# A weight transfer issued in nine pieces, and a bank of another group for two sums

## The chip, the cores and the metric

The kernel runs on one core of one Trainium2 chip. What counts is the time of one execution on the device, in microseconds (us). It is one kernel for two layers, a sliding-window attention and a spectral mixing layer behind it, and reads 163.58 MB from HBM, nearly all of it the weights of the second layer.

## The reference

The inputs are q, k and v of shape (8, 8, 576, 64), in float32, two sets of 64 matrices of 512x512 (`w_r`, `w_i`, 64 MB each) and one matrix `w_ch` of 512x512.

```python
# attention: causal, each row sees the 64 latest positions
scores = where(0 <= i - j < 64, q @ k.T / sqrt(64), -1e9)
x = softmax(scores) @ v                 # to (8, 576, 512)
# spectral mixing, 64 lowest modes of 576 positions
X = rfft(x, axis=1);  Xr, Xi = X.real[:, :64], X.imag[:, :64]
Yr = einsum('bmd,mde->bme', Xr, w_r) - einsum('bmd,mde->bme', Xi, w_i)
Yi = einsum('bmd,mde->bme', Xr, w_i) + einsum('bmd,mde->bme', Xi, w_r)
y = irfft(Yr + 1j * Yi, n=576)          # the other modes are zero
u = x + y
out = u + maximum(u @ w_ch, 0)
```

## The kernel before

The order of all work is written out by hand (a manual schedule): each engine runs its instructions in the order in which the Python code emits them. Semaphores between engines and transfers are put in by the framework.

**The weights** are streamed in bf16, cast on the way by transfers that GpSimd issues. `steps` is the list of groups of modes. For the first `EARLY` = 10 groups of four modes a step takes half of the rows (`hb`), so there are 20 such steps, ten with `hb` 0 and then ten with `hb` 1. After them come 12 steps of two whole modes each for the groups 10 to 15, two steps a group. Each step needs two transfers, `wr` and `wi`, `wlist` holds them in order, and `load_weights(n)` issues as many as it is allowed to. A transfer of the first 20 steps goes out at L178: 128 partitions, each with 4 modes of 2x512 values, 2 MB in HBM and 1 MB as it lands. Those of the last 12 steps go out at L169 and are of the same size; the last one of all is cut in three. A transfer needs a free buffer: `ringA` (3), `ringB` (5, the first 20 steps alone) or one of several lent tiles (`x_sb`, `Yfour`, `XQ`, `Yall`), and a buffer is free when the matmuls that read it are done. GpSimd's queue also carries q, k and v (L247) and `w_ch` (L1087), each in its place among the weights.

**The matmuls** of a step stand at L198 (`mode_half`, the first 20 steps) and L216 (`mode_pair`), 8 or 16 for each transfer. They add up in a PSUM tile `psm` of group "m"; DVE copies the sum out (L686, L709).

**While the weights come in**, the attention runs (until about 160 us). From then on, between two halves of a step, a list of jobs (`jobs`, `advance`) does what can be done ahead: `x @ w_ch` for all rows (`x_jobs`: transposes L639, matmuls L646, copies L867), and at the end, when the modes of the first 14 groups are there, for each batch `b` its inverse transform: `batch_job` (transposes into "t" at L762, ACT's copy L763, matmuls L646, ACT's copy L767), and for batches 0 to 3 `early_jobs`: `early_u`, which makes rows of `u` ahead (matmuls L825 and L826, then DVE's add L832 for odd tiles and ACT's copy L836 for even ones), and `add_late` (L811, L813). After the last weights the rows of the output are finished and sent out.

**PSUM** has eight banks: groups "m" (2), "t" (2), "y" (1), "p" (1) and "z" (2). `bank(group)` hands out the banks of a group in rotation; a new tile waits for the readers of the one that had the bank before. The two even sums of a batch (tiles 0 and 2, one job) take the banks "y" and "p" for batches 0 and 1, and both banks of "t" for batches 2 and 3.

Of the kernel before, what the change touches and what calls it, by code (L numbers as in the profile page):

```python
# [26 lines left out]
def kernel(  # L27
# [10 lines left out]
    nc = tc.nc  # L38
# [10 lines left out]
    HALF = DM // 2  # L49
    NJ = 2  # L50
# [6 lines left out]
    def pool(name, bufs=1, **kw):  # L57
        opened.append(tc.alloc_tile_pool(name=name, bufs=bufs, **kw))
        return opened[-1]
# [32 lines left out]
    EARLY = 10  # L92
    yp = pool("yp", side="right", reuse_waits="tile")
# [8 lines left out]
    XA = XA[:, 0:(3 * NW + 2) * B * NMF].rearrange("p (s b m) -> p s b m", b=B, m=NMF)  # L102
    steps += [(grp, hb) for grp in (*range(EARLY, LAST), *range(LAST + 2, NGRP), LAST, LAST + 1) for hb in range(2)]
    ONES = 3, 0
    wlist = []
    for at, (grp, hb) in enumerate(steps):
        for ri in range(2):
            p = 4 * grp
            if (at, ri) == ONES:
                parts = [[(p, p + 1)], [(p + 2,)], [(p + 3,)]]  # L110
# [33 lines left out]
    def load_weights(n):  # L144
        nonlocal nload
        while nload < len(wlist):
            at, parts, hb, ri = wlist[nload]
            if 2 * n <= sum(len(ps) for ps in parts):
                return
            if nload in lent:  # L150
                w = lent[nload]
            else:
                open_to = "a" if at >= 2 * EARLY else "aby" if at < EARLY + 2 else "ab"
                h = min(open_to, key=lambda h: held[h][0] if len(held[h]) == room[h] else -1)
                if len(held[h]) == room[h]:
                    if held[h][0] not in spent:
                        return
                    held[h].pop(0)
                held[h].append(nload)
                if h == "y":  # L160
                    w = lentY
                else:
                    w = {"a": ringA, "b": ringB}[h].tile([128, 4, NJ, DM], BF16, name="wi" if ri else "wr", tag="wt")
            src = moe_w_i if ri else moe_w_r
            if at >= 2 * EARLY:
                w = w.rearrange("p (m h) j e -> p m (h j) e", m=2)
                p = parts[0][0]
                for m, k, lo, hi in ((0, 1, 0, NW), (1, 1, 0, NJ), (1, 1, NJ, NW)) if nload == len(wlist) - 1 else ((0, 2, 0, NW),):
                    nc.gpsimd.dma_start(  # L169
                        out=w[:, m:m + k, lo:hi],  # L170
                        in_=src[p + m:p + m + k].rearrange("m (p j) e -> p m j e", j=NW)[:, :, lo:hi])
                wtiles.update(((p + m, ri), w[:, m]) for m in range(2))
                nload += 1
                n -= 2
                continue
            to = 0
            for ps in parts:
                nc.gpsimd.dma_start(  # L178
                    out=w[:, to:to + len(ps)],
                    in_=src[ps[0]:ps[-1] + 1, HALF * hb:HALF * hb + HALF, :].rearrange("g (p j) e -> p g j e", j=NJ))  # L180
                for i, p in enumerate(ps):
                    wtiles[p, hb, ri] = w[:, to + i]
                to += len(ps)
            nload += 1
            n -= to
# [38 lines left out]
    with tc.manual_schedule():  # L224
# [177 lines left out]
        at = scratch[:, 3 * NTC * NM:3 * NTC * NM + NTC]  # L402
# [6 lines left out]
        for nm in ("k", "q", "v"):  # L409
            load(1, nm)  # L410
        LEAD = 4
        load_weights(LEAD)
        nc.gpsimd.iota(Kb, pattern=[[64, NBLK]], base=0, channel_multiplier=0,
                       allow_small_or_imprecise_dtypes=True)
# [82 lines left out]
        def early_step(it):  # L497
            nonlocal step
            grp = step
            psm = ps_m.tile([128, DM], FP32, name="psm", tag="misc")  # L500
            for ri in range(2):
                mode_half(psm, grp, ri)
                load_weights(due(it) - loaded())
            nc.scalar.copy(out=Yacc[grp], in_=psm)
            step += 1
# [4 lines left out]
        for it in range(-3, NU + 3):  # L510
# [23 lines left out]
            g = starts.get(it + 2)  # L534
# [3 lines left out]
            g = starts.get(it + 1)  # L538
            if g is not None and g + 2 < NG:
                load(g + 2, "v")  # L540
            if it >= 0:
                for f in trig[0:2]:
                    f()
                del trig[0:2]
            load_weights(due(it) - loaded())
        do_dft(NG - 1)
        while step < EARLY:
# [24 lines left out]
        def bank(h, shape=(128, DM), dtype=FP32, name=None):  # L572
            return banks[h].tile(list(shape), dtype, name=name or "ps" + h, tag="bank")
# [56 lines left out]
        def yrows(b):  # L630
            return Yall[:, b, :]
# [184 lines left out]

        def early_u(b, cs):
            def done(_):
                pus = [bank("yp"[j] if b < 2 and len(cs) == 2 else "t") for j in range(len(cs))]
                for c, pu in zip(cs, pus):  # L820
                    i = tile_of(b, c)
                    at = tiles[i][1][0][0]
                    halves = pu.rearrange("p (h e) -> p h e", h=2)
                    if c % 2 == 0:
                        nc.tensor.matmul(out=halves, lhsT=ident_bf, rhs=tiles[i][0], start=True, stop=False)  # L825
                    nc.tensor.matmul(out=pu, lhsT=trigI[:, at:at + 128], rhs=yrows(b), start=(c % 2 == 1),  # L826
                                     stop=True)
                for c, pu in zip(cs, pus):
                    i = tile_of(b, c)
                    if c % 2:  # L830
                        UE[i] = spare[2 * b + c // 2]
                        nc.vector.tensor_tensor(out=UE[i].rearrange("p (h e) -> p h e", h=2),  # L832
                                                in0=pu.rearrange("p (h e) -> p h e", h=2), in1=tiles[i][0], op=ALU.add)
                    else:
                        UE[i] = x_sb[:, c // 2, b].rearrange("p c e -> p (c e)").bitcast(FP32)
                        nc.scalar.copy(out=UE[i], in_=pu)  # L836

            jobs.append((lambda: None, done))
# [19 lines left out]
        def tile_of(b, c):  # L858
            return 9 * (b // 2) + 4 * (b % 2) + c
# [24 lines left out]
        ps, pu = {}, {}  # L884
# [251 lines left out]
        for g in (2, 3):  # L1136
            nc.sync.dma_start(out=Zall.bitcast(FP32)[rows, 2 * g:2 * g + 2],
                              in_=ZL.bitcast(FP32)[32 * g:32 * g + 32])
# [43 lines left out]
```

## Time and profile before

| | |
|---|---|
| median of 3 runs | 432.17 us (431.64 to 432.29) |
| the profiled execution | 432.25 us |
| its span in the profile | 430.4 us |
| granted TensorE clock, mean | 0.886 |
| PE / DVE / ACT / POOL busy | 328.2 / 239.5 / 182.6 / 103.4 us |
| bytes moved, mean rate | 93.28 MB, 217 GB/s |
| weight transfers at L178, issue to landing | 13.6 / 21.7 / 38.6 us (least, median, most) |

All times inside the kernel are counted from the start of the span. PE is TensorE's matmuls, DVE VectorE, ACT ScalarE, POOL GpSimd, SP SyncE. A row of the timeline gives the start, the duration, the engine, the line of the code and the operation with the tile that it writes and reads; in brackets at its end stands how long the engine had been idle and what ended that. A transfer's issue on POOL is a row of its own (`DMA_DIRECT2D`); the transfer itself lands later.

### The profile page before, as it was taken

How to read it: one execution, taken by the hardware profiler on the slowest of the kernel's cores; microseconds unless marked ns; L12 is line 12 of the kernel's file. 1: busy time of each engine (PE TensorE's matmuls, PEld its weight loads, DVE VectorE, ACT ScalarE, POOL GpSimd, SP SyncE). 2: the span in 40 equal slices, each digit the busy share in tenths (PEclk: the TensorE clock that was granted, in tenths of full speed). 3: DMA queues.
4: the chain of work that ended last, by engine and by line, in shares of the span. 5: the costliest groups of instructions: out<-in, count | busy, mean ns of one | idle time of the engine just before them, and what ended most of it. 6: DMA issues, size and time to landing. Idle time of an engine off the chain costs nothing.

```text
span 430.4 us, 11413 instructions
## 1 busy us (share of the span) xinstructions
PE 328.2 (76%) x4962; PEld 220.9 (51%) x5006; DVE 239.5 (56%) x509; ACT 182.6 (42%) x330; POOL 103.4 (24%) x153
## 2 busy tenths in 40 slices
PE   6888989898999999974317344677587657979994
PEld 3666767676767676652104122345464445445552
DVE  8588877877577776876103112132222223874995
ACT  6566757575666667532201101114131213423663
POOL 8223222222122141112112100011111111120894
PEclk8699999999999999998556868559986999999998
DMA  8999999999999999999999999999999999995698
GB/s 205 211 211 212 211 213 209 211 212 212 211 211 212 212 212 210 212 212 212 212 257 214 212 211 212 215 214 214 212 215 214 209 215 213 214 211 95 226 372 301
DMA packets 40818, 93.28 MB, mean 217 GB/s; under 512 B 2528, under 2 KB 2784, under 8 KB 40768
## 3 DMA queue, kind: packets, MB, share of 16 engines
q0 software_dynamic: 35056, 81.80, 98.7%
q1 hardware_dynamic: 5568, 10.62, 6.7%
q8 instruction: 39, 0.64, 0.5%
q10 hardware_dynamic: 144, 0.13, 0.1%
q14 instruction: 11, 0.09, 0.1%
HBM read 163.58 MB, written 9.44 MB: 402 GB/s over the span
## 4 chain that ended last, share of the span: by engine, by line
DMA 49%; PE 37%; issue 6%; ACT 3%; DVE 3%; POOL 1%; DVEq 0%; POOLq 0%
DMA wi<-in_moe_w_i_dram 29%; DMA wr<-in_moe_w_r_dram 19%; PE tr L260 6%; PE s L307 4%; PE s L319 3%; PE pt L327 3%; PE vb L272 3%; PE o L347 2%; PE s L299 2%; PE psm L216 2%; PE psz L646 2%; PE psm L198 1%; PE pst L901 1%; DMA vd<-in_k_dram 1%; PE psz L901 1%
## 5 line engine op out<-in xcount | busy, mean ns | idle before, releaser
L646 PE MATMUL psz<-wch,tr 128*128 128x512 f32 x176 | 63.2, 490 | 11.7 <-DMA wch<-in_moe_w_ch_dram 10.9
L867 DVE CAST xw<-psz 128x512 fp32r<-128x512 f32 x36 | 24.9, 692 | 80.7 <-PE psz L646 80.7
L311 DVE TENSOR_REDUCE mx<-s 128x4 fp32r<-128x512 f32 x72 | 49.5, 688 | 25.8 <-PE s L307 25.5
L614 ACT CAST tr<-ptx 128x512 fp32r<-128x512 bf16 x36 | 21.2, 590 | 92.1 <-PE ptx L639 92.1
L646 PEld LDWEIGHTS psz<-wch,tr 128*128 128x128 f32 x176 | 36.8, 232 | 19.6 <-issue 11.3
L321 ACT ACTIVATE p<-s 128x512 bf16<-128x512 f32 x72 | 39.7, 603 | 13.5 <-PE s L319 13.5
L198 PEld LDWEIGHTS <-XQ 128*32 128x32 bf16 x320 | 13.0, 175 | 44.9 <-issue 27.3
L307 PE MATMUL s<-kT,qT 64*64 64x128 bf16 (+1 forms) x576 | 29.4, 223 | 6.9 <-issue 6.9
L264 ACT COPY kT<-tr 128x576 bf16<-128x576 bf16 x32 | 23.2, 725 | 21.5 <-PE tr L260 21.5
L198 PE MATMUL psm<-wi,XQ 128*32 128x512 bf16 x144 | 14.5, 478 | 20.7 <-DMA wi<-in_moe_w_i_dram 20.7
L264 ACT COPY qT<-tr 128x576 bf16<-128x576 bf16 x32 | 23.3, 728 | 11.0 <-PE tr L260 11.0
L330 DVE COPY pts<-pt 128x1024 bf16<-128x1024 bf16 (+1 forms) x40 | 25.2, 630 | 4.2 <-PE pt L327 2.7
L307 PEld LDWEIGHTS <-qT 64*64 64x64 bf16 x576 | 18.2, 108 | 18.0 <-issue 17.6
L319 PE MATMUL s<-mx,ident_r 128*128 128x512 f32 x72 | 26.8, 445 | 0.0
L686 DVE TENSOR_TENSOR stg<-psm,Yfour 128x512 bf16<-128x512 f32 x10 | 6.9, 690 | 35.4 <-PE psm L198 32.3
L169 POOL DMA_DIRECT2D wr<-in_moe_w_r_dram x12 | 8.4, 697 | 73.4 <-PE psm L216 37.4
L178 POOL DMA_DIRECT2D wi<-in_moe_w_i_dram x18 | 13.6, 754 | 51.2 <-PE psm L198 34.4
L264 ACT COPY vT<-tr 128x576 bf16<-128x576 bf16 x32 | 23.3, 728 | 4.1 <-PE tr L260 4.0
L247 POOL DMA_DIRECT2D rawk<-in_k_dram x15 | 8.1, 538 | 70.5 <-PE tr L260 64.2
L327 PE MATMUL pt<-ident_bf,p 128*128 128x128 bf16 x288 | 23.3, 220 | 1.5 <-issue 1.3
L216 PEld LDWEIGHTS <-XQ 128*32 128x32 bf16 x256 | 9.4, 151 | 28.4 <-issue 26.0
L198 PE MATMUL psm<-wr,XQ 128*32 128x512 bf16 x120 | 11.9, 477 | 15.7 <-DMA wr<-in_moe_w_r_dram 15.1
(257 smaller groups left out, 678.2 us busy)
## 6 DMA issues: line engine op xcount, KB each, us to landing
wi<-in_moe_w_i_dram POOLq DMA_DIRECT2D x29, 1024.0 KB, 18.4
wr<-in_moe_w_r_dram POOLq DMA_DIRECT2D x27, 1024.0 KB, 17.0
out_dram<-ut SPq DMA_DIRECT2D x29, 256.0 KB, 2.7
rawv<-in_v_dram POOLq DMA_DIRECT2D x16, 288.0 KB, 15.0
rawk<-in_k_dram POOLq DMA_DIRECT2D x15, 288.0 KB, 13.1
rawq<-in_q_dram POOLq DMA_DIRECT2D x15, 288.0 KB, 13.1
x_sb<-in_moe_w_r_dram POOLq DMA_DIRECT2D x2, 1024.0 KB, 15.9
out_dram<-utx SPq DMA_DIRECT2D x6, 256.0 KB, 2.3
```

Of the source, the lines that this page charges most:

```text
L198: nc.tensor.matmul(out=psm[32 * g:32 * g + 32, :], lhsT=XQ[hb].rearrange("k s b m -> k (s b) m")[:, (3 * j + 1 - ri) * B:(3 * j + 5 - ri) ...
L260: nc.tensor.transpose(out=pt[ro, j, :], in_=raw[ro, TH * half + j, :], identity=ident_bf[ro, ro])
L264: nc.scalar.copy(out=to, in_=pt.rearrange("p j n -> p n j"))
L307: nc.tensor.matmul(out=s[ro, t, lo:128], lhsT=lq, rhs=kT[ro, 64 * n - 64 + lo:64 * n + 64], start=False, stop=True, skip_group_check=True)
L311: nc.vector.tensor_reduce(out=mx, in_=s, axis=AX.X, op=ALU.max, negate=True)
L319: nc.tensor.matmul(out=s, lhsT=ident_r, rhs=mx.unsqueeze(2).to_broadcast([128, 4, 128]), start=False, stop=True, skip_group_check=True)
L321: nc.scalar.activation(out=p[:, 4 * c2:4 * c2 + 4, :], in_=s, func=ACT_F.Exp, scale=EX_SCALE)
L327: nc.tensor.transpose(out=pt[:, t, :], in_=st[u]["p"][:, t, :], identity=ident_bf)
L330: nc.vector.tensor_copy(out=ps[:, 0:nt, :], in_=pt[:, 0:nt, :])
L614: nc.scalar.copy(out=tr, in_=pt)
L646: nc.tensor.matmul(out=pz, lhsT=tr[:, c, :], rhs=wch[:, c, :], start=(c == 0), stop=(c == NDCH - 1))
L867: nc.vector.tensor_copy(out=XW[i], in_=multiply(tr))
```

## The change

There are two edits, which have nothing to do with each other.

The `wr` transfer of step 14 (group 4, second half of the rows) is no longer one issue of 128 partitions. It becomes eight issues of two partitions each (0-1, 2-3, up to 14-15) and one of the partitions 16 to 127. The bytes and where they go are the same; the issues follow each other on GpSimd's queue, in the place of the one.

In `early_u` the two even sums of batches 2 and 3 take one bank of "t" and one of "m", not two of "t".

```diff
     ONES = 3, 0
+    IN_PAIRS, NPAIR = (EARLY + 4, 0), 8
     wlist = []
...
             to = 0
+            cuts = [*range(0, 2 * NPAIR, 2), 2 * NPAIR, 128] if (at, ri) == IN_PAIRS else [0, 128]
             for ps in parts:
-                nc.gpsimd.dma_start(
-                    out=w[:, to:to + len(ps)],
-                    in_=src[ps[0]:ps[-1] + 1, HALF * hb:HALF * hb + HALF, :].rearrange("g (p j) e -> p g j e", j=NJ))
+                of = src[ps[0]:ps[-1] + 1, HALF * hb:HALF * hb + HALF, :].rearrange("g (p j) e -> p g j e", j=NJ)
+                for lo, hi in zip(cuts, cuts[1:]):
+                    nc.gpsimd.dma_start(out=w[lo:hi, to:to + len(ps)], in_=of[lo:hi])
                 for i, p in enumerate(ps):
                     wtiles[p, hb, ri] = w[:, to + i]
                 to += len(ps)
...
         def early_u(b, cs):
             def done(_):
-                pus = [bank("yp"[j] if b < 2 and len(cs) == 2 else "t") for j in range(len(cs))]
+                pus = [bank(("yp" if b < 2 else "tm")[j] if len(cs) == 2 else "t") for j in range(len(cs))]
```

## The prediction

> **What bounds the kernel now.** I read the page first: its slices, its queues and the shares of the chain that ended last.
>
> ```profile
> DMA  8999999999999999999999999999999999995698
> GB/s 205 211 211 212 211 213 209 211 212 212 211 211 212 212 212 210 212 212 212 212 257 214 212 211 212 215 214 214 212 215 214 209 215 213 214 211 95 226 372 301
> q0 software_dynamic: 35056, 81.80, 98.7%
> DMA 49%; PE 37%; issue 6%; ACT 3%; DVE 3%; POOL 1%; DVEq 0%; POOLq 0%
> ```
>
> The DMA engines are full from the first slice to the 36th, at one rate. So until about 396 us the end is set by the weight stream, all of it on GpSimd's queue q0; the 34 us after that are PE's, DVE's and POOL's. A change in the stream moves the end by what it does to the stream's last landing.
>
> Next I read GpSimd's timeline around the split transfer, which is issued at 186.77 us.
>
> ```profile
> 178.85 0.75 POOL L178 DMA_DIRECT2D wr<-in_moe_w_r_dram  x1
> 186.03 0.74 POOL L178 DMA_DIRECT2D wi<-in_moe_w_i_dram  x1 [6.44 <-PE psm L198]
> 186.77 0.75 POOL L178 DMA_DIRECT2D wr<-in_moe_w_r_dram  x1
> 195.06 0.74 POOL L178 DMA_DIRECT2D wi<-in_moe_w_i_dram  x1 [7.55 <-PE psm L198]
> ...
> 200.27 0.86 POOL L178 DMA_DIRECT2D wi<-in_moe_w_i_dram  x1 [2.98 <-DMA wr<-in_moe_w_r_dram]
> 205.27 0.74 POOL L178 DMA_DIRECT2D wr<-in_moe_w_r_dram  x1 [4.15 <-DMA wi<-in_moe_w_i_dram]
> 210.21 0.74 POOL L178 DMA_DIRECT2D wi<-in_moe_w_i_dram  x1 [4.19 <-DMA wr<-in_moe_w_r_dram]
> 215.12 0.74 POOL L178 DMA_DIRECT2D wr<-in_moe_w_r_dram  x1 [4.17 <-DMA wi<-in_moe_w_i_dram]
> ```
>
> From 200 us on an issue waits for a DMA, not for a free buffer. In the program as built, every transfer from GpSimd waits for one of eight landing semaphores in rotation, so for the landing of the transfer eight places before it. The trace agrees: those landed at 199.74, 204.74, 209.68 and 214.59, and the issues above start 0.53 after each. At most eight transfers are in flight, whatever their size. PE's timeline shows three of these landings (PE starts 0.04 to 0.05 after them), and that a later wait is for wch:
>
> ```profile
> 204.79 1.11 PE L198 MATMUL psm<-wi,XQ 128*32 128x512 bf16 x8 [4.10 <-DMA wi<-in_moe_w_i_dram]
> 209.72 1.11 PE L198 MATMUL psm<-wr,XQ 128*32 128x512 bf16 x8 [3.28 <-DMA wr<-in_moe_w_r_dram]
> 214.63 1.11 PE L198 MATMUL psm<-wi,XQ 128*32 128x512 bf16 x8 [3.47 <-DMA wi<-in_moe_w_i_dram]
> 227.21 1.19 PE L646 MATMUL psz<-wch,tr 128*128 128x512 f32 x2 [10.94 <-DMA wch<-in_moe_w_ch_dram]
> ```
>
> Each transfer leaves sixteen landing marks in the trace, one for each engine. For the transfer that landed at 214.59 the first mark is at 209.20: eight engines lie within 1.34 of it, eight come 3.46 to 5.38 later. The late eight have the same rate as the others (4.95 us a transfer) and are late because the instruction fetches (q8, 0.88 to 0.98 us each, 39 of them) take turns on eight engines. Their work sets every "last landing".
>
> Last, the end of the chain of waits:
>
> ```profile
> 361.68 14.56 DMA wi<-in_moe_w_i_dram
> ...
> 376.28 0.69 PE psm L216 x16
> ...
> 386.79 0.59 ACT x_sb L836
> 387.39 0.04 issue
> 387.43 0.38 PE ptx L762 x4
> ...
> 395.52 0.80 PE psm L216 x16
> ```
>
> After the landing at 376.24 the chain runs over DVE, PE and ACT, and meets the stream again at its very end: the last piece lands at 395.84, and the last matmuls of L216, which PE began at 395.45, go on without a gap. The two are level there, so an earlier PE alone gains nothing, and a later landing is paid in full.
>
> **The change, part by part.** *The pairs.* One issue becomes nine, so eight more on POOL. Each costs about 0.53 (L178 with one row a partition: 0.53; with four: 0.75), in all 4.2 us, and POOL was idle for 7.55 before its next issue: the issue time itself is covered. The waits are not. In flight before the split transfer are the eight issued at 157.22, 159.93, 160.66, 168.38, 169.11, 178.12, 178.85 and 186.03, which landed at 179.21, 184.63, 189.87, 194.78, 199.74, 204.74, 209.68 and 214.59. Pair 1 waits for the first of these (and for its buffer, 186.77 as now), pair 2 for the second, pair 8 for the last. So pair 8 can't be issued before 214.59 + 0.53 = 215.12, and by then every whole transfer has left the queue. Behind it on POOL stand the piece of 112, the wi of 195.06, wch of 195.79, and all weights after them; PE waits for these. That is the cost: the stream runs dry.
>
> The restart, for the latest engine, which finished at 214.59: pair 8 is issued 215.12 to 215.65; the piece of 112 follows at 215.65 (it waits only for pair 1, long queued and landed by then or up to 0.6 later if that pair sat on a late engine). From issue to first packet there are two rows. The small copies Yall<-stg, issued at 398.72 into an idle queue, show their first packet at 399.83, 1.11 later; the first transfer of the kernel, issued at 1.74, shows it at 4.94, 3.20 later. I take the warm one and add 0.20, since the issue is that much longer (0.75 against 0.55): 216.96. The first packets of the kernel took up to 1.34 where the usual one takes 0.19; I take 0.4 for this (bounds 0 and 1.15): 217.4. Then 112 partitions are 7 for an engine instead of 8, 28 packets of 4.95/32 = 0.155: 4.33, so it lands at 221.7. The split transfer landed at 219.54. The stream is 2.15 late. Bounds: 215.57 + 1.11 + 4.33 = 221.0, so 1.5; and 215.65 + 3.20 + 1.15 + 4.33 = 224.3, so 4.8.
>
> The fixed cost of a queued transfer from GpSimd is put at about 2.0 us by the Trainium skill (DMA: Bandwidth & Descriptors, Anatomy of one DMA); by it the sum would be 215.65 + 2.0 + 4.33 = 221.98, so 2.4 late. No run here shows that figure by itself.
>
> Does the loss come back? The early engines lose 5.4 more, for they stood still since 209.2, but their lead was worth nothing: all sixteen start level at 217.4, and each of the eight late ones gets one more instruction fetch before 396 as it does now (233.7, 275.3, 299.9, 315.5, 335.2, 354.6, 374.2 and 393.9, in turn). From 219.54 to 395.84 the latest engine needs 176.3 us before and after. Starting level takes 0.5 off the landing at 376.24 (there a fetch hit an engine already late), but not off the last one. Refilling costs nothing: the next issues follow at 0.75 apart, each for 4.95 us of work, and their buffers are free, since PE has used everything up to 214.63 and waits. wch, landed at 227.08, comes at about 229.2, and PE waits that much longer at L646. So the last piece lands at about 398.0, and PE, long there, goes on 2.15 later.
>
> *The banks.* In the jobs of batches 2 and 3 the second even sum moves from "t" to "m". PE's order stays; two waits go. For batch 2 (ACT L836 at 379.36) DVE is busy without a break from 377.42 to 380.94, so nothing moves. For batch 3 the transposes at 387.43 waited for ACT's copy of 386.79 to 387.39; now they can follow the sums, at about 386.8, 0.6 sooner. The banks of "m" that it takes were read long before, and the next pair's sums, at 382.17, get the one that L709 read at 376.99. The cover for this 0.6 is the stream: with the last piece at 395.84 or later, PE only waits longer for it. I count 0; without that cover it would be 0.6 less.
>
> Sum: 432.25 (the profiled execution, 430.4 of span and 1.85 around it) + 2.15 = 434.4. The median of the runs is 0.08 lower, so 434.3.
>
> **The rivals.** *A, the pairs pile up on two engines.* Which engines serve two partitions, no row shows. I assumed that all eight pairs are through before the piece of 112 starts. If all eight go to the same two and one of these is a late one, that engine has 8 x 0.62 = 4.95 to do after 214.59, then 4.33 for its share of the 112: 223.9, 4.35 late, 436.5. It decides where 4.95 exceeds the dry stretch of 2.8. For it: eight of sixteen engines are late. Against: even then two early engines would have done it by 214.2.
>
> By the Trainium skill (DMA: Bandwidth & Descriptors, Why a DMA increments its semaphore by 16 and not by 1) two partitions run on two consecutive engines from a round-robin cursor, which spreads eight pairs over all sixteen; it also tells of direct copies with the rounded-up sixteenth of the partitions on each engine from the first on, which would put them all on the first two. No run here shows which holds.
>
> *B, no dry stretch.* If the wait for the landing eight places back does not bind pair 8, the pieces queue behind 214.59 as the whole did, the late engines do 7 partitions instead of 8 wherever a pair lands on an early one, and the last landing comes up to 0.62 sooner; PE's 0.6 from the banks then counts too. 431.6: not slower, and within the noise. It decides if the piece of 112 goes out before about 213.3 (214.59 less the 1.31 to its first packet). Against it: four issues in a row start 0.53 after exactly that landing.
>
> *C, the loss is absorbed.* If the end after 376 were PE's alone, a late stream would be hidden and the time stay at 432.2. Against: the last matmuls go on within 0.04 of the last landing, so the slack is nil.
>
> **How the numbers follow.** The dry stretch, 433.7 to 435.5: 0.70. A: 0.12. B and C, both inside the 0.2% (0.86 us, 431.3 to 433.0) that a measurement of this kernel can tell from no change: 0.10. Faster by more has no mechanism in these rows, since the late engines can't save more than one partition; 0.08 for what they don't show. The range 432.9 to 436.8 holds the first two cases and leaves out nearly all of the rest. Faster 0.08, same 0.10, slower 0.82.
>
> **What would show it.** In GpSimd's timeline: pairs issued at about 186.8, 187.3, 190.4, 195.3, 200.3, 205.3, 210.2 and 215.1, each but the first two 0.53 after a landing, and the piece of 112 at 215.7. A dip in the page's DMA and GB/s rows in the 20th and 21st slices; sixteen landing marks within about 1 us after it; wch at L646 at about 229.3; the last L216 about 2 us later. If the rows of GB/s show no dip there, the forecast is wrong; if the marks show two engines 2 us behind the rest, it is A.

## The result, and the profile after

| | before | after |
|---|---|---|
| median of the runs | 431.93 us (4 runs, 431.64 to 432.29) | 435.58 us (4 runs, 435.47 to 437.43) |
| the profiled execution | 432.25 us | 435.47 us |
| its span | 430.4 us | 433.7 us |
| granted TensorE clock, mean | 0.886 | 0.883 |

The ratio is 1.0094, with a 95% interval of 1.0065 to 1.0123: slower by 3.65 us, where 2.15 was forecast.

The lines of the code have moved by 1 to 4 (the transfer of L178 is L182 now, the matmuls of L198 are L200, L216 is L218, L646 is L648, L762 is L764). First the page: its slices (10.8 us each), its weight queue and the shares of the chain that ended last.

```profile
DMA  8999999999999999999699999999999999996698
GB/s 204 211 212 212 212 213 209 211 212 211 211 212 211 212 212 210 212 212 212 119 202 249 211 212 212 213 215 215 214 215 214 215 213 215 215 214 137 218 365 308
q0 software_dynamic: 35632, 81.80, 98.0%
DMA 46%; PE 35%; issue 9%; DVE 3%; ACT 3%; POOL 2%; DVEq 0%; POOLq 0%
```

The hole in the stream is the 20th slice: 119 GB/s where 212 is usual. The peak that stood in the 21st slice before (257) is in the 22nd now (249). It is no catching up: it is the slice in which wch comes in, which lands as many bytes in 2.5 us as a weight transfer in 4.95, and it moved with wch. The bytes are the same, in 576 more packets. `issue`, time in which the chain waits for nothing that the profile shows, rises from 6% to 9% of the span.

GpSimd's timeline from the first pair on (start, duration, engine, line, operation; in brackets the idle time before and what ended it):

```profile
187.21 0.74 POOL L182 DMA_DIRECT2D wi<-in_moe_w_i_dram  x1 [6.43 <-PE psm L200]
187.94 1.11 POOL L182 DMA_DIRECT2D wr<-in_moe_w_r_dram  x2
190.08 0.54 POOL L182 DMA_DIRECT2D wr<-in_moe_w_r_dram  x1 [1.03 <-DMA Yall<-in_moe_w_r_dram]
194.99 0.54 POOL L182 DMA_DIRECT2D wr<-in_moe_w_r_dram  x1 [4.37 <-DMA wi<-in_moe_w_i_dram]
199.94 0.54 POOL L182 DMA_DIRECT2D wr<-in_moe_w_r_dram  x1 [4.42 <-DMA wr<-in_moe_w_r_dram]
204.95 0.54 POOL L182 DMA_DIRECT2D wr<-in_moe_w_r_dram  x1 [4.47 <-DMA wi<-in_moe_w_i_dram]
209.88 0.54 POOL L182 DMA_DIRECT2D wr<-in_moe_w_r_dram  x1 [4.39 <-DMA wr<-in_moe_w_r_dram]
214.80 1.25 POOL L182 DMA_DIRECT2D wr<-in_moe_w_r_dram  x2 [4.38 <-DMA wi<-in_moe_w_i_dram]
216.04 0.79 POOL L182 DMA_DIRECT2D wi<-in_moe_w_i_dram  x1
```

Every pair from the third on waits for a landing, the last for the wi of 187.21, which lands at 214.51. The row of 214.80 is two issues, pair 8 and, at 215.33, the piece of 112. The wi behind it, which had gone out at 195.06 before, goes out at 216.04.

What PE meets, in its timeline:

```profile
214.56 1.11 PE L200 MATMUL psm<-wi,XQ 128*32 128x512 bf16 x8 [3.48 <-DMA wi<-in_moe_w_i_dram]
231.20 2.04 PE L648 MATMUL psz<-wch,tr 128*128 128x512 f32 x4 [14.99 <-DMA wch<-in_moe_w_ch_dram]
```

The last whole transfer comes when it did (214.63 before). wch comes 3.99 later than before (227.21), and PE's idle time ahead of it grows from 10.94 to 14.99.

The end of the chain of waits (start, duration, what):

```profile
365.52 14.66 DMA wi<-in_moe_w_i_dram
380.22 0.69 PE psm L218 x16
...
394.55 2.09 PE psz L648 x8
396.67 0.59 ACT Zall L769
397.30 0.50 PE psz L813
397.81 0.61 PE psm L218 x16
398.84 0.83 PE psm L218 x16
```

The chain is the one of before, 3.94 later at 380.22 and 3.32 later at the last L218 (398.84 against 395.52). The landing marks say the same of the stream: the last piece is there at 399.19, against 395.84.

### The profile page after: what moved, and what is told of

Read it like the earlier page. It is cut to its first block, busy times and chain, and to the rows that moved or that the text cites. A ratio compares the mean times of both kernels' runs of the same rounds, so it can differ in the third digit from the quotient of the medians.

```text
span 433.7 us, 11428 instructions
## 1 busy us (share of the span) xinstructions
PE 328.8 (76%) x4962; PEld 221.1 (51%) x5006; DVE 239.2 (55%) x509; ACT 182.4 (42%) x330; POOL 107.6 (25%) x161
## 4 chain that ended last, share of the span: by engine, by line
DMA 46%; PE 35%; issue 9%; DVE 3%; ACT 3%; POOL 2%; DVEq 0%; POOLq 0%
DMA wi<-in_moe_w_i_dram 34%; DMA wr<-in_moe_w_r_dram 11%; PE tr L262 6%; PE s L309 4%; PE s L321 3%; PE pt L329 3%; PE vb L274 3%; PE o L349 2%; PE s L301 2%; PE psz L648 2%; PE psm L218 2%; PE psm L200 2%; DMA vd<-in_k_dram 1%; PE pst L903 1%; PE px L372 1%
## 5 line engine op out<-in xcount | busy, mean ns | idle before, releaser
L648 PE MATMUL psz<-wch,tr 128*128 128x512 f32 x176 | 62.9, 489 | 15.9 <-DMA wch<-in_moe_w_ch_dram 15.0
L648 PEld LDWEIGHTS psz<-wch,tr 128*128 128x128 f32 x176 | 36.9, 233 | 23.7 <-issue 15.4
L200 PEld LDWEIGHTS <-XQ 128*32 128x32 bf16 x320 | 13.1, 176 | 43.7 <-issue 28.2
L200 PE MATMUL psm<-wi,XQ 128*32 128x512 bf16 x144 | 15.3, 495 | 20.8 <-DMA wi<-in_moe_w_i_dram 20.8
L170 POOL DMA_DIRECT2D wr<-in_moe_w_r_dram x12 | 8.4, 697 | 75.3 <-PE psm L218 41.5
L182 POOL DMA_DIRECT2D wr<-in_moe_w_r_dram x23 | 15.7, 683 | 34.1 <-DMA wi<-in_moe_w_i_dram 13.2
L218 PEld LDWEIGHTS <-XQ 128*32 128x32 bf16 x256 | 9.2, 150 | 28.7 <-issue 27.0
L200 PE MATMUL psm<-wr,XQ 128*32 128x512 bf16 x120 | 12.4, 479 | 14.0 <-DMA wr<-in_moe_w_r_dram 13.3
```

The lines of the kernel that those rows point to most:

```text
L200: nc.tensor.matmul(out=psm[32 * g:32 * g + 32, :], lhsT=XQ[hb].rearrange("k s b m -> k (s b) m")[:, (3 * j + 1 - ri) * B:(3 * j + 5 - ri) ...
L648: nc.tensor.matmul(out=pz, lhsT=tr[:, c, :], rhs=wch[:, c, :], start=(c == 0), stop=(c == NDCH - 1))
```

## Experiments

All times are medians; the last column but one is the ratio to runs of the kernel before on the same chip (their medians: 432.07 to 432.23 us). "Split lands" is the last landing mark of the step-14 `wr`, in one piece or many, and "last piece" that of the last weights.

| | us | ratio (95%) | split lands / last piece |
|---|---|---|---|
| before | 431.93 | | 219.54 / 395.84 |
| after | 435.58 | 1.0094 (1.0065 to 1.0123) | 223.52 / 399.19 |
| banks alone | 431.79 | 0.9992 (0.9981 to 1.0003) | not split / 395.31 |
| pairs alone | 435.92 | 1.0081 (1.0059 to 1.0103) | 223.41 / 399.10 |
| seven issues | 432.35 | 1.0003 (0.9991 to 1.0016) | 219.44 / 395.85 |
| eight issues | 435.22 | 1.0061 (1.0040 to 1.0082) | 222.73 / 398.89 |
| eight equal pieces | 431.96 | 0.9999 (0.9989 to 1.0008) | 219.79 / 395.36 |
| cut at two steps | 439.77 | 1.0176 (1.0161 to 1.0191) | 223.23, then 269.47 / 403.10 |
| ten transfers cut | 437.24 | one run | / 400.94 |
| held whole | 435.53 | 1.0071 (1.0049 to 1.0093) | 223.24 / 399.09 |
| held whole, then a gap | 437.20 | 1.0101 (1.0079 to 1.0122) | 223.76 / 400.66 |

In ten of the eleven profiled executions the span ends 34.4 to 34.6 us after the landing of the last piece (with the pairs alone 35.1). So what a kernel loses is what its weight stream loses.

My theory: at most eight of GpSimd's transfers are in flight, small pieces take the places of large ones, the queue runs dry, and the restart is the loss. The rivals were that the banks matter, that the pairs do harm by themselves (as nine issues, or by piling up on two engines), and that the engines' lost lead, not the restart, is what costs.

**Banks alone**: the kernel before with this one edit.

```diff
-                pus = [bank("yp"[j] if b < 2 and len(cs) == 2 else "t") for j in range(len(cs))]
+                pus = [bank(("yp" if b < 2 else "tm")[j] if len(cs) == 2 else "t") for j in range(len(cs))]
```

> The banks alone, the transfer whole. My theory (the loss is the dry stretch of the weight stream): no change, 431.3 to 432.4, since PE and the last landing stand level at the end; the transposes of batch 3 at L764 (387.4 in the kernel before) start some 0.6 us sooner and PE waits longer for the last piece. Rival (the banks carry part of the loss of 3.65 us, by a new wait for a bank of group m): slower by 1 us or more.

PE's timeline of this kernel:

```profile
386.54 0.39 PE L762 MATMUL ptx<-ident_bf,Yall 128*128 128x128 bf16 x4
394.57 1.22 PE L216 MATMUL psm<-wi,XL 128*32 128x256 bf16 x16
```

The transposes that stood at 387.43 start 0.89 sooner and with no idle time before them, so the wait for ACT's copy is gone. The last matmuls start 0.88 sooner too (395.45 before) and then take 1.22 instead of 0.87, since they wait in mid-row for the last piece. They end at 395.79, 0.48 after the last piece (395.31), as they did before (396.32, with the piece at 395.84): the stream sets the end of both. The profiled span is 429.8. The interval of the ratio holds 1: no change that this measurement can tell.

**Pairs alone**: the changed kernel with the old banks.

```diff
-                pus = [bank(("yp" if b < 2 else "tm")[j] if len(cs) == 2 else "t") for j in range(len(cs))]
+                pus = [bank("yp"[j] if b < 2 and len(cs) == 2 else "t") for j in range(len(cs))]
```

> The pairs alone, the banks as before. My theory: the whole of the loss, 435.0 to 436.2, with the dip of the stream between 209 and 218 us. Rival (banks carry part of it): under 434.7.

435.92, and the intervals of this and of both edits overlap. The whole loss is the pairs'. PE's timeline has one thing more:

```profile
391.33 0.38 PE L764 MATMUL ptx<-ident_bf,Yall 128*128 128x128 bf16 x4 [0.46 <-ACT x_sb L838]
399.36 0.69 PE L218 MATMUL psm<-wi,XL 128*32 128x256 bf16 x16
```

The old wait for ACT is back, and the last matmuls start only after the last landing (399.10) and end 0.95 after it. In the ten other kernels they end 0.48 or 0.49 after it. So with the old banks PE ended some 0.5 us behind the stream in this execution; the times do not tell the two kernels apart (435.92 and 435.58).

**Seven and eight issues**: the same partitions cut less often. With seven, the large piece takes the place before the last whole one lands; with eight, it has to wait for that landing.

```diff
# seven issues
-            cuts = [*range(0, 2 * NPAIR, 2), 2 * NPAIR, 128] if (at, ri) == IN_PAIRS else [0, 128]
+            cuts = [0, 2, 4, 6, 8, 12, 16, 128] if (at, ri) == IN_PAIRS else [0, 128]
# eight issues
+            cuts = [0, 2, 4, 6, 8, 10, 12, 16, 128] if (at, ri) == IN_PAIRS else [0, 128]
```

> The same 16 partitions cut in 2, 2, 2, 2, 4, 4, then the 112: seven issues for nine, banks as in the changed kernel. My theory (at most eight transfers in flight): the piece of 112 then waits for the landing at about 209.6 and goes out at about 210, before the late engines are done at 214.5, so the late engines never stand still: 431.3 to 432.6, no dip below about half in the DMA row. Rival (each small piece costs the stream something of its own, 4 us over eight pieces): 434 to 435.

> One issue more than the kernel called seven: pieces of 2, 2, 2, 2, 2, 2, 4, then the 112. My theory: the piece of 112 waits for the last whole transfer, the landing at about 214.5, and goes out at about 214.8, some 0.5 us sooner than with nine issues: 434.6 to 435.4, so nearly all of the loss comes with this one issue. Rival (a price for each piece): halfway between, about 434.7 with seven at 434.2.

GpSimd's timeline of the kernel with seven issues, the large piece and the transfer behind it:

```profile
209.65 0.72 POOL L182 DMA_DIRECT2D wr<-in_moe_w_r_dram  x1 [4.38 <-DMA wr<-in_moe_w_r_dram]
214.87 0.78 POOL L182 DMA_DIRECT2D wi<-in_moe_w_i_dram  x1 [4.50 <-DMA wr<-in_moe_w_r_dram]
```

The same of the kernel with eight:

```profile
214.79 0.72 POOL L182 DMA_DIRECT2D wr<-in_moe_w_r_dram  x1 [4.33 <-DMA wr<-in_moe_w_r_dram]
215.50 0.78 POOL L182 DMA_DIRECT2D wi<-in_moe_w_i_dram  x1
```

And the GB/s of the page, first with seven issues, then with eight:

```profile
GB/s 209 212 211 211 211 212 212 211 211 211 212 211 212 212 212 211 212 212 212 188 223 221 212 212 212 215 214 215 214 214 215 215 214 213 215 214 130 225 375 299
```

```profile
GB/s 203 211 212 211 212 211 211 211 212 212 211 212 211 212 213 210 212 212 212 126 216 242 212 212 212 215 214 216 214 214 214 214 215 214 215 214 129 219 375 299
```

One issue more moves the large piece from 209.65 to 214.79 and costs 2.87 us (435.22 less 432.35); the ninth adds nothing that can be told. So it is neither the number of issues nor the two-partition pieces, but the place in the rotation that the large piece gets. Seven are free because the large piece then enters a queue in which the late engines still have nearly five microseconds of work (the wi ahead of it lands at 214.32). The early engines do fall back: the first landing mark of the large piece comes at 216.48, where that of the whole transfer came at 214.16 before, and their lost lead costs nothing at the end. The next wi lands 0.87 late (225.43 against 224.56), 0.48 of this is still there at the landing of 385.89 (385.41 before), and at the last piece it is gone; where it goes is told below.

**Eight equal pieces**: as many issues as the kernel that lost 3 us, but of 16 partitions each.

```diff
-            cuts = [*range(0, 2 * NPAIR, 2), 2 * NPAIR, 128] if (at, ri) == IN_PAIRS else [0, 128]
+            cuts = [*range(0, 129, 16)] if (at, ri) == IN_PAIRS else [0, 128]
```

> The split transfer as eight pieces of 16 partitions, banks as in the changed kernel: as many issues as the kernel called eight (435.2 us), and its last piece too can go out only after the landing at about 214.5. My theory (the late engines must run dry for a loss): at 214.5 they still have seven pieces, 4.3 us of work, so they don't stand still: 431.5 to 433.0. Rival (the number of places taken is what counts, wherever the bytes are): 434.8 to 435.6.

GpSimd's timeline:

```profile
209.70 0.51 POOL L182 DMA_DIRECT2D wr<-in_moe_w_r_dram  x1 [4.43 <-DMA wr<-in_moe_w_r_dram]
214.61 0.51 POOL L182 DMA_DIRECT2D wr<-in_moe_w_r_dram  x1 [4.41 <-DMA wi<-in_moe_w_i_dram]
215.56 0.76 POOL L182 DMA_DIRECT2D wi<-in_moe_w_i_dram  x1 [0.45 <-PE psm L200]
```

The last piece goes out as late as the large one did with eight unequal cuts (214.61 against 214.79), and the time is that of the kernel before. Each of the seven pieces issued earlier held an eighth of the work, so the late engines were still busy with them when the eighth was issued. What counts is the work in the eight places, not how many they are.

**Cut at two steps**: the `wr` of step 18 is cut in the same way as that of step 14.

```diff
-            cuts = [*range(0, 2 * NPAIR, 2), 2 * NPAIR, 128] if (at, ri) == IN_PAIRS else [0, 128]
+            cuts = [*range(0, 2 * NPAIR, 2), 2 * NPAIR, 128] if (at, ri) in (IN_PAIRS, (EARLY + 8, 0)) else [0, 128]
```

> A second transfer (step 18, wr) is cut like the first, eight pairs and 112; the queue runs dry again some 47 us later, now with engines that stand nearly level. My theory (each dry stretch costs its restart, 3 to 4 us): 438.0 to 439.8. Rival (the loss of the first is the lead of the early engines, which can be lost only once): 435.6 to 436.6.

GpSimd's timeline at the second place:

```profile
255.76 0.54 POOL L182 DMA_DIRECT2D wr<-in_moe_w_r_dram  x1 [4.37 <-DMA wr<-in_moe_w_r_dram]
260.86 1.25 POOL L182 DMA_DIRECT2D wr<-in_moe_w_r_dram  x2 [4.56 <-DMA wi<-in_moe_w_i_dram]
```

The pattern repeats. The last whole transfer lands at 260.58, the piece of 112 goes out at 261.39 and lands at 269.47, where the next whole transfer would have landed at 260.58 + 4.95 = 265.53: 3.94 late. The first is 3.69 late here (223.23 against 219.54) and 3.98 in the changed kernel. The time is 4.19 over that of after, and the last piece comes 3.91 later. At the second place the sixteen engines were already within 1.6 us of each other, so there was no lead left to lose. The rival "lost lead" is refuted; each dry queue costs its restart.

**Ten transfers cut**, to learn which engines are the late ones: the `wr` and `wi` of steps 12 to 16 each go out as four pieces of eight partitions by modes, and one of 112.

```diff
-    IN_PAIRS, NPAIR = (EARLY + 4, 0), 8
+    SKEW = EARLY + 2, EARLY + 7
...
-                for lo, hi in zip(cuts, cuts[1:]):
-                    nc.gpsimd.dma_start(out=w[lo:hi, to:to + len(ps)], in_=of[lo:hi])
+                parted = [(0, 8, 0, 4), (8, 16, 0, 1), (8, 16, 1, 3), (8, 16, 3, 4), (16, 128, 0, 4)]
+                for lo, hi, m, k in parted if SKEW[0] <= at < SKEW[1] else [(0, 128, 0, len(ps))]:
+                    nc.gpsimd.dma_start(out=w[lo:hi, to + m:to + k], in_=of[lo:hi, m:k])
```

> For a version that beats both: the ten weight transfers of steps 12 to 16 are issued as 8 partitions of four modes, 8 of one, the same 8 of two and of one, and the 112, banks as in the changed kernel. If a piece of eight partitions goes to eight consecutive engines and the next piece to the other eight, one half of the engines gets 0.31 us less work a transfer and the other 0.31 more, 3.1 us in all. If the eight late engines are the relieved half: the last landing about 2.5 to 3 us sooner and 429 to 430. If they are the loaded half: 434.5 to 435.5, and the reverse would gain. If late and early engines are mixed in both halves, or pieces go elsewhere: 432 to 435.5, with marks that spread further.

437.24 in a single run, 400.94 for the last piece. Five issues a transfer leave some 1.6 transfers in the eight places, and the stream ran thin (165 to 202 GB/s in five slices, where 212 is usual). The engines did come closer together, but by the early ones falling back. It doesn't tell the halves apart: a miss for its purpose, and one more case of the eight places.

**Held whole**: the sum above had been off in its restart, and this kernel measures the restart by itself. The `wr` of step 14 is one issue again, but GpSimd first copies a column of the wi before it into a small new tile (`hush`, 128x64), and so waits for the same landing as pair 8.

```diff
-            cuts = [*range(0, 2 * NPAIR, 2), 2 * NPAIR, 128] if (at, ri) == IN_PAIRS else [0, 128]
+            cuts = [0, 128]
+            if (at, ri) == IN_PAIRS:
+                nc.gpsimd.tensor_copy(out=hush[:, 0:1], in_=wtiles[4 * steps[at - 1][0], steps[at - 1][1], 1][:, 0, 0:1])
```

> No pieces at all: the wr of step 14 goes out whole, but GpSimd first copies one column of the wi before it (the transfer that lands at 214.6), so that the issue waits for that landing as pair 8 did. Banks as in the changed kernel. Theory (the loss is the dry queue, not the pieces): issued at about 214.8; from issue to last landing the piece of 112 took 8.19 us in the changed kernel, and one partition more an engine is 0.62, so it lands at about 223.6, 4.0 late, and the time is 435 to 436.5. Rival (the pieces add to it): the restart goes as I forecast, first packet 1.31 to 1.41 after the issue, 0.4 of ramp, 4.95 of work: landed at about 221.5, 2.0 late, time 433.5 to 434.3.

GpSimd's timeline:

```profile
186.36 0.74 POOL L185 DMA_DIRECT2D wi<-in_moe_w_i_dram  x1 [6.44 <-PE psm L203]
214.72 0.18 POOL L181 CAST hush<-wi 128x1 f32<-128x1 bf16 x1 [27.62 <-DMA wi<-in_moe_w_i_dram]
215.21 0.75 POOL L185 DMA_DIRECT2D wr<-in_moe_w_r_dram  x1 [0.30 <-issue]
215.94 0.75 POOL L185 DMA_DIRECT2D wi<-in_moe_w_i_dram  x1
```

435.53: 3.30 over its own runs of before, without a single small piece; the interval of the ratio overlaps that of the changed kernel. The first sixteen packets start 1.45 to 1.74 after the issue (216.66 to 216.95). With 4.95 of work behind the first packet the transfer would be there at 216.66 + 4.95 = 221.61; the first engine is done at 222.60, the median at 222.92 and the last at 223.24. So here the ramp is 1.0 to 1.6 us, 1.3 at the median. The early packets show it: the first sixteen take 0.21 to 0.81 us and single later ones up to 1.15, where the usual one takes 0.173.

**Held whole, then a gap**: the same, and behind the held issue GpSimd does 16 small memsets before it issues anything else.

```diff
                     nc.gpsimd.dma_start(out=w[lo:hi, to:to + len(ps)], in_=of[lo:hi])
+                if (at, ri) == IN_PAIRS:
+                    for _ in range(16):
+                        nc.gpsimd.memset(hush, 0.0)
```

> As hold, and GpSimd then does 16 small memsets (some 2.3 us) before it issues the next transfers, so that the held one is alone in the queue while it starts; its 4.95 us of work cover the gap, if the next is issued by 218. If what slows the restart is the issues that follow at 0.75 us each (they use the same queue), the held transfer lands 1 to 2 us sooner than in hold and the time is that much less, 433.5 to 434.5. If the slow start is the transfer's own, it lands within 0.3 us of hold's and the time is the same as hold's or up to 1 us more.

GpSimd's timeline, then the page's GB/s:

```profile
215.16 0.75 POOL L185 DMA_DIRECT2D wr<-in_moe_w_r_dram  x1 [0.30 <-issue]
215.89 3.31 POOL L188 MEMSET hush<- 128x64 f32 x16
219.54 0.74 POOL L185 DMA_DIRECT2D wi<-in_moe_w_i_dram  x1 [0.34 <-issue]
```

```profile
GB/s 206 211 211 212 211 212 212 210 212 212 211 213 210 212 212 211 212 213 211 100 187 257 211 212 212 214 213 215 214 215 215 213 216 212 216 213 137 214 372 303
```

Alone in the queue the held transfer is no faster: its median engine is done at 222.81 (222.92 without the gap), its last at 223.76. That is 0.52 later than without the gap, outside the 0.3 that I had named, and not the 1 to 2 us sooner of the other case. So the issues that follow don't make the restart slow. The gap itself came out longer than planned, 3.31 us and not 2.3, and the next issue, at 219.54, was 3.3 us ahead of the median engine's end of work. Even so there is a second hole: 15 to 22 packets start in each half microsecond from 222.5 to 223.5, where some 50 are usual, and single ones take 1.14 us. That transfer ends 5.88 after the one before it, not 4.95, and the time is 1.67 over the held one's. My "up to 1 us more" was too little.

No version beats the kernel before. The banks alone, the seven issues and the eight equal pieces are level with it within their intervals.

## Why the prediction was right, and where its sum was short

**The mechanism held.** Pair 8 waits for the landing eight places before; the issues were forecast at 186.8, 187.3, 190.4, 195.3, 200.3, 205.3, 210.2 and 215.1 and came at 187.9, 188.5, 190.1, 195.0, 199.9, 205.0, 209.9 and 214.8. The piece of 112 came at 215.33 (215.65 forecast), since pair 8 went out 0.29 after the landing, not 0.53. The first packet of it, forecast at 216.96, came at 216.74. From 214.67 to 216.3 no engine starts a packet with data. That it is this place in the rotation is shown by seven against eight issues, and that it is the dry queue by the held kernel.

**The step that was mis-sized is the ramp**, "I take 0.4 for this (bounds 0 and 1.15)". With the 4.33 of the piece's own work the median engine should be done at 216.74 + 4.33 = 221.07 and is done at 222.2, 1.1 later; four engines come 0.9 to 1.3 behind that, the last at 223.52, 2.45 later. So this term is 1.1 to 2.45 instead of 0.4, and the loss at this transfer 3.98 instead of 2.15. The 0.4 had been picked between its bounds without a row of its own, and the landing goes by the last engine, not by a usual one. The other price of the restart, from issue to first packet, was close: 1.41, where the sum had 1.31.

Not all of the 1.1 is slow packets. Before the change a landing mark comes 0.34 us (median) after the start of the 4-byte packet that closes a transfer on its engine, and the sum has no term for this. That leaves 0.8 at the median engine. The packets account for it: between 216 and 223 us, what they take beyond the usual 0.173 adds up to 0.7 us an engine, where it was nothing before. Why four engines of sixteen pay more is open: with eight issues there are four as well (0.8 to 0.9 behind the median of 221.8), without a pair just before, and in the held kernel there are none.

The Trainium skill (DMA: Bandwidth & Descriptors, Anatomy of one DMA) puts the fixed cost of such a transfer at about 2.0 us, which made 2.4 late in the estimate on record. The trace has 1.4 from issue to first packet and, with the 1.1 of the median engine, about 2.5; the page's figure was nearer than my 1.71 and still short of the last engine.

**"Starting level takes 0.5 off the landing at 376.24, but not off the last one"** had it the wrong way round. At 376.24 the delay is 3.94, so nothing of the 3.98 is back: the instruction fetch of 378.1 leaves one engine 0.97 behind the next there, as that of 374.2 left one 0.87 behind before. At the last piece the delay is 3.35, and this 0.63 does not come from the level start. At the landing of 385.41 the delay is still 3.93; it falls to 3.35 within the next transfer. Before the change that one landed 5.47 after its forerunner, at 390.88, and now it takes 4.89 (394.23). In the kernel before, single packets took up to 1.34 us between 384.9 and 390.2, where 0.32 is usual for them; now none takes over 0.43. The pieces behind that transfer had been issued 2.0 us ahead of the first engine's end of work (383.07 and 385.11), and now 4.8 (387.01 and 391.81). That this lead is the reason is not shown. So "From 219.54 to 395.84 the latest engine needs 176.3 us before and after" failed too: it needs 175.67 after the change, because the kernel before has a slow stretch of its own in this execution. The seven issues lose their last 0.48 in the same place. The span follows the last piece, 3.3 longer.

**The banks, counted at 0**, are 0 (0.9992, 0.9981 to 1.0003). The wait went as described, 0.9 sooner instead of 0.6, and in the kernel with this edit alone PE waits for the last piece instead. Beside the pairs they may be worth up to 0.5, by the trace of the pairs alone: once the stream has won back its 0.63, a PE with the old banks is the later of the two. The times don't show it.

**Rival A**, pairs piled up on two engines, is wrong. The marks of pair 8 are within 0.13 us on fourteen engines, and two more follow 1.1 to 1.3 later, as engines with data would. From the wi ahead of the pairs to the seventh pair the sixteen marks, taken in order, move by 1.1 to 2.4 us; an engine that had to do all seven would have moved by 7 x 0.62 = 4.3. The Trainium skill's round-robin cursor (DMA: Bandwidth & Descriptors, Why a DMA increments its semaphore by 16 and not by 1) agrees with these marks, and its exception with the rounded-up sixteenth doesn't. **Rival B**, no dry stretch, is wrong for nine issues; it is what seven issues do, at 432.35. **Rival C**, the loss absorbed, is wrong: 3.35 at the last piece and 3.3 of span.

**The range** reached far enough because its upper end came from the coldest row for issue to first packet (3.20) and from rival A, and neither happened; in that it held by luck. The ramp, which did, had a bound of 1.15 and would not have filled the range by itself: with it the landing would have been at 222.4, and the last engine was at 223.52.

## What to carry to other kernels

Where a queue allows a fixed number of transfers in flight, count the work in those places: a small piece takes a whole place, and a large one behind seven small ones comes to an empty queue. Before a transfer is cut, work out when the last piece may be issued and whether the slowest engine still has work then; seven unequal or eight equal pieces cost nothing here, eight unequal ones 3 us. A stream that runs dry costs more than the dry time to the first packet: price the restart until the last engine is back at its steady rate.

## What the runs showed of the hardware

- A dry weight queue took 8.0 us from issue to last landing for 4.95 us of work: 1.45 to the first packet, and 1.0 to 1.6 of ramp (0.34 of it the usual lag of the landing mark), with packets of up to 1.15 us instead of 0.173. The median engine was done at the same time whether other issues followed at once or 4.4 us later (222.92 and 222.81).
- The queue need not be dry to be slowed. A transfer issued 3.3 us ahead of the median engine's end of work still cost 0.9 us more than the usual 4.95, and with seven issues the next wi, issued at 214.87 with work ahead of it until 219.44 on the last engine, landed at 225.43 where the same one landed at 224.56 before. Why is open; in this stream of 4.95 us a transfer, an issue 4.6 us ahead of the last engine's end of work was not always enough.
- A transfer of two partitions leaves sixteen landing marks like a whole one: for pair 8 fourteen at 216.24 to 216.37 and two at 217.46 and 217.65.
